# Waits on TensorE's own work behind 256-instruction borders, also at units that already wait for two operations

## The chip, the cores and the metric

The kernel runs on one core of a Trainium2 chip. The metric is the device time of one execution in microseconds; the median of the runs is compared, and one execution is profiled.

## The reference

Two layers run one behind the other on 2048 rows of width 512, in bfloat16.

```
h  = x + attention(layernorm(x), mem0, Wq, Wk, Wv, Wo)     # 64 segments of 32 rows, a recurrence
h2 = h + (gelu(layernorm(layernorm(h)) @ w1 + b1) @ w2 + b2)

for s in range(64):                       # 32 heads of 128 each
    hs = concat(mem, x[32*s : 32*s+32])   # 8 rows of memory, 32 rows of the segment
    q, k, v = hs@Wq, hs@Wk, hs@Wv
    p = softmax(mask(q k^T * 128**-0.5))
    o = (p v) @ Wo
    mem, out[s] = o[:8], o[8:]            # the memory rows go into the next segment
```

The 64 segments are a chain, as each needs the eight memory rows of the one before. The second layer needs only finished rows.

## The kernel before

**Units and streams.** The program builds no instruction directly. It records operations (here called units on TensorE: a small group of weight loads and matmuls), each with what it reads and writes and an estimated duration. `schedule` orders them by a simulation of the five engines with their dependences; `wire` gives each operation the list `waits`, the operations of other engines or DMAs whose semaphores it must wait for; `windows` delays some transfers that SyncE issues; `pauses`, the subject of this document, comes last. `emit` then writes each engine's stream: for each entry in `waits` a `wait_ge`, then the instructions of the unit, the last of which counts up the engine's semaphore if anybody waits for the unit.

**How a wait becomes an instruction.** In the built program the first wait of a TensorE unit's list rides on the unit's first weight load or matmul. The others stand ahead of it in semaphore instructions (the profile shows them as EVENT_SEMAPHORE at L627, the line of `wait_ge`), each of which holds two. One wait takes no semaphore instruction, two or three take one, four or five two: `len(o.waits) // 2`, as `align` counts them.

**The work of a segment on TensorE.** The names are those of the order tables in the kernel. Q0, K0, Q1, K1, V0 and V1 are the projections, in passes of 8 instructions, four passes each (L970 and L709; a pass takes 0.2157 us in the plan). SC0 and SC1 (L1167, 32 instructions) are scores of the memory's rows, for heads 0 to 15 and 16 to 31; VectorE and ScalarE make a softmax of them, which VectorE transposes into `PTC` (L1184). F is filler: work that doesn't depend on the recurrence (projections of later rows, the second layer's W1, the late rows' Wo). PV0 and PV1 (L1198, L1202, 20 instructions) multiply `PTC` by V, PVA (L1274, L1280, 40 instructions) does it for the segment's own rows. WO (L1314) is eight units of 16 instructions. SA (L1224, 64 instructions) makes the scores of the next segment's own rows. SC0 waits for VectorE's transpose of K (`KALL`, L1010) and for a copy of Q into `ZC` (L1039, mostly on GpSimd); PV0 and PV1 wait for `PTC` and for an evacuation of V (`VS`, ScalarE).

**Borders.** TensorE's instructions come from memory in pieces of 256; in this kernel a border lies behind every 256th instruction of its stream, counted from a fixed offset (`FETCH_AT`). `pads` inserts weight loads without effect, so that the borders fall at chosen units. `align` walks the stream, counts the instructions and the waits' semaphore instructions, and puts into `heads` the first unit that starts behind each border.

**Pauses.** Behind each border `pauses` goes through the units that begin within the next `PAUSE_IN` = 64 instructions. To up to `PAUSES` = 3 of them it gives a wait on TensorE's own semaphore: on the latest earlier TensorE unit that ends, in the plan, at least `PAUSE_US` = 0.5 us before the unit starts. Before the change it does so only at units that wait for nothing else: passes, filler and WO units, but not SC0, PV0, PV1 or PVA, each of which waits for two operations or more. In this kernel there are 153 borders and 423 such waits.

Of the kernel before, what the change touches and what calls it, by code (L numbers as in the profile page):

```python
# [160 lines left out]
class Sched:  # L161
# [230 lines left out]
    def pauses(self):  # L392

        self.align()
        pe = self.streams["pe"]
        ends = [o.start + o.dur for o in pe]
        for first in self.heads:
            n, i = 0, first
            while n < PAUSES and i < len(pe) and pe[i].at < pe[first].at + PAUSE_IN:
                o = pe[i]  # L400
                j = bisect.bisect_right(ends, o.start - PAUSE_US) - 1
                if not o.waits and 0 <= j < i:
                    o.waits = [pe[j]]
                    pe[j].sig = True
                    n += 1
                i += 1
        c = 0
        for o in pe:
            if o.sig:
                c += 1  # L410
                o.sigcount = c
# [1463 lines left out]
```

## Time and profile before

| what | value |
|---|---|
| three runs | 783.87, 784.82, 785.61 us; median 784.82 |
| the profiled execution | 784.86 us, of which 783.1 us is the span of the trace |
| granted TensorE clock in it | 1.00 |

Times in the views are microseconds from the start of the span. A row of the timeline is: start, duration, engine, line of the kernel, operation, what it writes and reads with shapes, and the number of instructions that the row stands for; in square brackets the idle time ahead of it and what ended it ("issue": nothing that the profile shows was waited for). PE is TensorE's matmul side, PEld its weight loads, PEldq semaphore instructions that stand ahead of weight loads, DVE VectorE, ACT ScalarE, POOL GpSimd, SP SyncE. A row of the semaphore instructions gives count, shortest/median/longest duration in ns, and when the first and the last of them started; a semaphore instruction is shown from the moment at which what it waits for is there. A row of the DMA queues gives the packets, the megabytes and the time that the packets took as a share of 16 engines; q8 is the queue that brings instructions.

### The profile page before, as it was taken

The numbers are of one execution on the slowest core, as the hardware profiler recorded it, in microseconds if no ns is written. First come the engines' busy times: TensorE is split into PE (matmuls) and PEld (weight loads), VectorE is DVE, ScalarE is ACT, GpSimd is POOL, SyncE is SP. The second block draws the span as 40 slices with busy tenths as digits, with TensorE's granted clock in tenths as the row PEclk, the third lists the DMA queues.
The fourth block names the chain that finished last, engine by engine and source line by source line (L and its number), as shares of the span: only waits on it lengthen the run. The fifth ranks groups of instructions, "written<-read, shape, count | busy, mean of one in ns | idle before, by whom it ended". The sixth has DMA issues, their size and how long they took to land.

```text
span 783.1 us, 44192 instructions
## 1 busy us (share of the span) xinstructions
PE 763.2 (97%) x19535; PEld 407.8 (52%) x19327; DVE 592.4 (76%) x1873; ACT 535.6 (68%) x1391; POOL 310.4 (40%) x830
## 2 busy tenths in 40 slices
PE   6979999999999999999999999999999999999898
PEld 2325555655655555655555555555555555554344
DVE  4458888888888888888888988888898777764311
ACT  3547777767677777777777777777767777776332
POOL 3012233444444444444444435443444434446600
PEclk9999999999999999999999999999999999999999
DMA  9973212020212111202020101111131120169510
GB/s 316 393 224 75 64 44 35 7 48 15 50 39 44 32 39 51 51 26 51 23 51 24 46 28 42 33 36 45 29 84 35 54 74 31 51 211 293 131 41 27
DMA packets 75915, 58.56 MB, mean 75 GB/s; under 512 B 31172, under 2 KB 68556, under 8 KB 75724
## 3 DMA queue, kind: packets, MB, share of 16 engines
q1 hardware_dynamic: 75392, 55.47, 25.2%
q8 instruction: 153, 2.51, 1.3%
q14 instruction: 38, 0.31, 0.1%
q10 hardware_dynamic: 332, 0.27, 0.1%
HBM read 37.63 MB, written 11.80 MB: 63 GB/s over the span
## 4 chain that ended last, share of the span: by engine, by line
PE 90%; SPq 6%; DVE 1%; DMA 1%; POOL 1%; issue 1%; ACT 0%; DVEq 0%; POOLq 0%
PE high L970 33%; PE high L709 17%; PE quad L1314 15%; PE quad L1743 4%; PE high L1521 3%; PE high L1353 3%; SPq L896 3%; PE high L1731 3%; SPq L871 2%; PE quad L1167 2%; PE quad L1224 2%; PE quad L1274 2%; PE quad L1198 2%; PE high L1198 1%; DMA WO<-in_A_Wo_dram 1%
## 5 line engine op out<-in xcount | busy, mean ns | idle before, releaser
L970 PE MATMUL high<-WQ,hT 128*32 128x512 bf16 x1796 | 156.3, 381 | 1.6 <-DVE hT L1320 1.2
L709 PE MATMUL high<-WK,hT 128*32 128x512 bf16 x1260 | 126.4, 379 | 0.2 <-issue 0.2
L988 ACT CAST kq<-high 128x512 bf16<-128x512 f32 x184 | 105.8, 583 | 30.0 <-PE high L970 18.4
L1314 PE MATMUL quad<-WO,OT 128*32 128x256 bf16 x4032 | 121.9, 273 | 0.0
L970 PE MATMUL high<-WV,hT 128*32 128x512 bf16 x1544 | 116.6, 379 | 0.0
L1247 POOL TENSOR_TENSOR PA<-SA,rsa 128x256 bf16<-128x256 f32 x64 | 39.6, 619 | 185.7 <-DVE rsa L1239 119.9
L1314 PEld LDWEIGHTS quad<-WO,OT 128*32 128x32 bf16 x4032 | 102.2, 97 | 5.3 <-issue 0.5
L989 ACT ACTIVATE kq<-high 128x512 bf16<-128x512 f32 x156 | 91.9, 598 | 15.6 <-PE high L970 12.4
L970 PEld LDWEIGHTS high<-WQ,hT 128*32 128x32 bf16 x1796 | 50.8, 95 | 73.1 <-issue 31.7
L1255 POOL COPY BD<-PTA 32x128 f32<-32x128 f32 x256 | 80.3, 314 | 16.3 <-DVE PTA L1251 0.6
L988 ACT CAST VS<-high 128x512 bf16<-128x512 f32 x127 | 73.7, 581 | 0.2 <-PE high L970 0.2
L1010 DVE STREAM_TRANSPOSE KALL<-kq 128x256 f32<-128x256 f32 x160 | 69.5, 435 | 4.1 <-ACT kq L988 1.2
L988 ACT CAST OT<-quad 128x384 bf16<-128x384 f32 (+1 forms) x126 | 47.2, 375 | 26.1 <-PE quad L1202 25.0
L1326 DVE STREAM_TRANSPOSE TT<-quad 128x256 f32<-128x256 f32 x63 | 28.3, 449 | 43.3 <-PE quad L1314 43.1
L1010 DVE STREAM_TRANSPOSE QT<-kq 128x256 f32<-128x256 f32 x128 | 54.8, 428 | 2.8 <-ACT kq L989 2.5
L970 PE MATMUL high<-WK,hT 128*32 128x512 bf16 x788 | 55.7, 379 | 1.0 <-DMA WK<-in_A_Wk_dram 1.0
L1050 ACT COPY KALL<-KALL 128x128 f32<-128x128 f32 x63 | 18.8, 298 | 53.0 <-PE quad L1224 51.8
L1366 POOL TENSOR_TENSOR opT<-TTB,TTS 32x64 bf16<-32x64 f32 x128 | 39.9, 312 | 37.1 <-DVE opT L1320 21.2
L968 PEld LDWEIGHTS <-hT 128*32 128x32 bf16 x2432 | 39.3, 96 | 27.9 <-DVE hT L1320 5.9
L1167 PEld LDWEIGHTS quad<-KALL,ZC 128*32 128x32 bf16 x1984 | 31.2, 96 | 43.0 <-POOL BD L1255 18.4
L709 PE MATMUL high<-WV,hT 128*32 128x512 bf16 x504 | 51.6, 379 | 0.0
L1182 DVE SCALAR_TENSOR_TENSOR PC<-EC,rsc,even 128x128 bf16<-128x128 f32 x126 | 46.4, 368 | 4.3
(204 smaller groups left out, 1588.0 us busy)
## 6 DMA issues: line engine op xcount, KB each, us to landing
WK<-in_A_Wk_dram SPq DMA_DIRECT2D x4, 1024.0 KB, 18.2
WQ<-in_A_Wq_dram SPq DMA_DIRECT2D x4, 1024.0 KB, 18.2
WO<-in_A_Wo_dram SPq DMA_DIRECT2D x16, 256.0 KB, 7.8
VBD<-v_last SPq DMA_DIRECT2D x60, 64.0 KB, 2.0
g_pre<-kq SPq DMA_DIRECT2D x14, 256.0 KB, 2.2
WV<-in_A_Wv_dram SPq DMA_DIRECT2D x3, 1024.0 KB, 11.3
VSB<-in_B_w_dram SPq DMA_DIRECT2D x44, 64.0 KB, 2.2
xr<-in_A_x_dram SPq DMA_DIRECT2D x17, 128.0 KB, 2.8
```

Source lines behind the costliest of these rows:

```text
L709: return e.add_instruction(mybir.InstMatmult(name="I-%d" % (4000000 + _kept[0]), engine=mybir.EngineType.PE, start_tensor_calc=start, stop ...
L968: e.ldweights(l, tile_position=(0, 32 * j))
L970: ins = e.matmul(o, l, m, start=(k == 0), stop=(k == DC - 1), tile_position=(0, 32 * j), skip_group_check=True)
L988: return {"act": (lambda e: e.copy(out, src), t_act(n, ps_)), "dve": (lambda e: e.tensor_copy(out, src), 0.155 + 1.0e-3 * n * fast)}
L989: return {"act": (lambda e: e.mul(out, src, scale_), t_act(n, ps_)), "dve": (lambda e: e.tensor_scalar(out, src, scale_, None, ALU.mult), ...
L1010: turn = lambda after: S.op("dve", lambda e: e.transpose(out, src), reads=[("kq", i)], writes=[key], dur=t_dve(256) + 0.02, after=after)
L1167: ins = e.matmul(o[32 * j:32 * j + 32, :], zc_window(h), rhs, start=False, stop=(i == 3), tile_position=(0, 32 * j), skip_group_check=True)
L1182: S.op("dve", lambda e: e.scalar_tensor_tensor(PC[:, r].rearrange("p k b -> p b k"), xc, rsc[:, r:r + 1], ev, ALU.mult, ALU.mult), reads=[ ...
L1247: S.either({k: ((lambda e: e.tensor_tensor(PA[:, 0:4].rearrange("p a t b -> p a b t"), SA[:, :, 0:SEG].rearrange("p (a b) t -> p a b t", b ...
L1255: S.narrow(S.op("pool", lambda e, j=j, rows=rows: e.tensor_copy(words(BD[rows, :, j, :, :]), words(PTA[rows, 0:4])), reads=["PTA"], writes ...
L1314: ins = e.matmul(ps[bank][32 * j:32 * j + 32, 0:256], lhs(slot(h)), wo_cols(h, b), start=(k == 0), stop=(k == 15), tile_position=(0, 32 * ...
L1366: return e.tensor_tensor(o[32 * q:32 * q + 32, c:c + 2], x, y, ALU.add)
```

## The change

In the profile's numbering the changed lines are in `pauses`:

```
             while n < PAUSES and i < len(pe) and pe[i].at < pe[first].at + PAUSE_IN:
                 o = pe[i]
                 j = bisect.bisect_right(ends, o.start - PAUSE_US) - 1
-                if not o.waits and 0 <= j < i:
-                    o.waits = [pe[j]]
+                if len(o.waits) % 2 == 0 and 0 <= j < i and not any(p.eng == "pe" and not p.is_dma for p in o.waits):
+                    o.waits = sorted(o.waits + [pe[j]], key=lambda p: p.start + p.dur + self.lat(p, o))
                     pe[j].sig = True
                     n += 1
```

A unit also gets the wait if it has two waits already (or four, or six), none of them on TensorE. The list with the new wait in it is sorted by the time at which each awaited operation is planned to be seen. The limit of three for each border stays, so a wait that is put on an earlier unit can take the place of one further on.

More of the change, by code (lines that the diff above doesn't have):

```diff
@@ L401, in pauses @@
                 j = bisect.bisect_right(ends, o.start - PAUSE_US) - 1
-                if not o.waits and 0 <= j < i:
-                    o.waits = [pe[j]]
+                if len(o.waits) % 2 == 0 and 0 <= j < i and not any(p.eng == "pe" and not p.is_dma for p in o.waits):
+                    o.waits = sorted(o.waits + [pe[j]], key=lambda p: p.start + p.dur + self.lat(p, o))
                     pe[j].sig = True
```

## The prediction

> **What bounds the kernel now.** I read the page first: the busy times, the chain that ended last, the DMA queues.
>
> ```profile
> span 783.1 us, 44192 instructions
> ...
> PE 763.2 (97%) x19535; PEld 407.8 (52%) x19327; DVE 592.4 (76%) x1873; ACT 535.6 (68%) x1391; POOL 310.4 (40%) x830
> ...
> q8 instruction: 153, 2.51, 1.3%
> ...
> PE 90%; SPq 6%; DVE 1%; DMA 1%; POOL 1%; issue 1%; ACT 0%; DVEq 0%; POOLq 0%
> ```
>
> TensorE is busy for 97% of the span and carries 90% of the chain; waits of other engines matter only through it. Queue q8 brings instructions: 153 packets of 2.51 MB / 153 = 16.4 KB, one for each border of the kernel's pieces (256 instructions at 64 bytes), each at work for 0.013 x 16 x 783.1 / 153 = 1.06 us. Then the windows view over the segments, and TensorE's timeline at one border inside them.
>
> ```profile
> 100.00:640.00 540.00, 538.85 (x15404) 299.52 (x15412) 462.34 (x1508) 397.54 (x1080) 233.22 (x640) 1.00 0.16 39
> ```
>
> ```profile
> 165.49 0.39 PE L709 MATMUL high<-WK,hT 128*32 128x512 bf16 x3
> 166.05 0.38 PE L709 MATMUL high<-WK,hT 128*32 128x512 bf16 x1 [0.17 <-issue]
> 166.09 0.55 PE L970 MATMUL high<-WQ,hT 128*32 128x512 bf16 x4
> ```
>
> In 540 us TensorE stands still for 1.15 us, at a granted clock of 1.00. So no wait for data is left to shorten there; what is left is stops like the one at 166.05: the stream reaches a border, nothing that a semaphore shows is late, and the next instruction comes late all the same ("issue"). The change touches nothing else that TensorE waits for, so its effect has to come through these stops, or through new stops of its own.
>
> **The change part by part.** It has three parts: 52 waits are added at 46 of the 153 borders (the lists walked by the new condition: 19 on SC0, 14 on PV1, 8 on PV0, 6 on PVA, 5 on single units at the two ends); 22 old ones fall out, since a border still gets three (17 on the third V0 pass behind an SC0); and the order of the waits at the changed units may shift.
>
> Instructions: none. A unit with two waits has one semaphore instruction ahead of it and one wait on its first weight load; the third wait goes into that same semaphore instruction, which holds two. So no border moves. I cost this at 0.
>
> SC0 (19). The unit at 455.80 stands for them.
>
> ```profile
> 454.94 0.83 PE L970 MATMUL high<-WK,hT 128*32 128x512 bf16 x12
> ...
> 455.80 0.31 PE L1167 MATMUL quad<-KALL,ZC 128*32 128x64 bf16 x16
> ```
> ```profile
> 455.00 0.45 DVE L1010 STREAM_TRANSPOSE KALL<-kq 128x256 f32<-128x256 f32 x1
> ```
> ```profile
> 455.04 0.29 POOL L1039 COPY ZC<-QT 128x128 bf16<-128x128 bf16 x1
> ```
>
> The added wait is on a unit inside the first row: the latest one that ends half a microsecond ahead of SC0 in the plan, about 455.34 by the trace. VectorE's transpose ends at 455.00 + 0.45 = 455.45, later. The wait is met before the old ones are: 0. The same holds for PV1, where the transposed PTC comes last, and for PVA, which stands behind PV0 in the stream.
>
> PV0 (8, seven of them with a fetch behind) is the exception.
>
> ```profile
> 171.47 0.40 PE L709 MATMUL high<-WK,hL 128*32 128x512 bf16 x4
> ...
> 171.90 0.40 PE L709 MATMUL high<-WK,hL 128*32 128x512 bf16 x4
> 172.23 0.26 PE L1198 MATMUL quad<-PTC,VS 64*128 64x16 bf16 x8
> ...
> 172.74 0.26 PE L1198 MATMUL high<-PTC,VS 64*128 64x16 bf16 x8
> ```
> ```profile
> 171.19 0.23 DVE L1184 STREAM_TRANSPOSE PTC<-PC 128x64 f32<-128x64 f32 x1
> ...
> 172.35 0.25 DVE L1184 STREAM_TRANSPOSE PTC<-PC 128x64 f32<-128x64 f32 x1
> ```
> ```profile
> L627 PEldq EVENT_SEMAPHORE  x3: 51/51/51, 171.4 to 171.7; - x3
> ```
> ```profile
> 109.30 0.40 PE L709 MATMUL high<-WV,hL 128*32 128x512 bf16 x4
> ```
> ```profile
> 109.23 0.24 DVE L1184 STREAM_TRANSPOSE PTC<-PC 128x64 f32<-128x64 f32 x1
> ```
> ```profile
> L627 PEldq EVENT_SEMAPHORE  x2: 51/51/51, 109.5 to 109.7; - x2
> ```
> ```profile
> 77.99 0.23 DVE L1184 STREAM_TRANSPOSE PTC<-PC 128x64 f32<-128x64 f32 x1
> ```
> ```profile
> 78.25 0.40 PE L709 MATMUL high<-WK,XX 128*32 128x512 bf16 x4
> ```
>
> At 172.23 the old wait, on PTC, is met at 171.19 + 0.23 = 171.42, and the gate (the semaphore instruction ahead of the unit) opens at 171.4. The new one, on the unit of 171.47, is met when that ends, 171.47 + 0.40 = 171.87: some 0.4 us later, 0.35 of it at the gate that opens last. At 110.06 the two ends are 109.47 and 109.70, and the gate opens 0.2 later; near 79, 78.22 and 78.65, 0.4 later. Of the seven, one is like 79, two like 172 (the other at 214) and four like 110 (141, 193 and 275 too, worked out in the same way): 0.4 + 2 x 0.35 + 4 x 0.2 = 1.9 us by which gates open later.
>
> Does this delay PV0 itself? A unit behind a gate can start 0.14 after its last operand is there: PTC's second half ends at 172.60 and PV1 starts at 172.74. The new gate opens 172.23 - 171.87 = 0.36 ahead of PV0, so the matmul is on time: 0 directly. Queued behind the wait on TensorE are PV0, PVA and the next projections; nobody else waits for them earlier than today.
>
> What the later gate may delay is the next fetch. The DMA queue view has no q8 packet in 109.7 to 110.6 nor in 171.8 to 172.6, and one in each of the next 0.2 us:
>
> ```profile
> q8 instruction: 1, 0.02, 30.7%
> ```
> ```profile
> q8 instruction: 1, 0.02, 38.3%
> ```
>
> These fetches start 1.1 to 1.2 us behind the first gate, as they do at the other five of these borders. If that is cause, each starts later by what its gate does. Who waits for it: the border after, in the SA unit that follows.
>
> ```profile
> 82.11 0.65 PE L1224 MATMUL quad<-KALL,QT 128*32 128x40 bf16 x32
> ```
> ```profile
> 113.09 0.40 PE L1224 MATMUL quad<-KALL,QT 128*32 128x40 bf16 x32
> ```
> ```profile
> 143.95 0.19 PE L1224 MATMUL quad<-KALL,QT 128*32 128x40 bf16 x4
> 144.39 0.36 PE L1224 MATMUL quad<-KALL,QT 128*32 128x40 bf16 x28 [0.25 <-issue]
> ```
> ```profile
> 175.17 0.69 PE L1224 MATMUL quad<-KALL,QT 128*32 128x40 bf16 x32
> ```
> ```profile
> 195.99 0.40 PE L1224 MATMUL quad<-KALL,QT 128*32 128x40 bf16 x32
> ```
> ```profile
> 216.92 0.41 PE L1224 MATMUL quad<-KALL,QT 128*32 128x40 bf16 x32
> ```
> ```profile
> 278.44 0.60 PE L1224 MATMUL quad<-KALL,QT 128*32 128x40 bf16 x32
> ```
>
> Undisturbed the unit takes 0.40. Four of the seven take 0.25, 0.40 (143.95 to 144.75), 0.29 and 0.20 more: those borders are already late, and take a later fetch whole: 0.4 + 0.2 + 0.35 + 0.2 = 1.15. The other three (113, 196, 217) have a slack that the trace does not show: between 0 and 0.2 + 0.2 + 0.35 = 0.75. I take 0.35, the middle, since the four neighbours show that the slack is small at best. Sum: 1.15 + 0.35 = 1.5, bounds 1.15 and 1.9.
>
> The 22 dropped waits. Seventeen are the third stop behind SC0; the first two V0 passes and SC0's gate keep theirs. Most of these fetches start 1.1 to 1.3 us behind SC0's gate, which stays: 0. Three start later, 282.8's among them:
>
> ```profile
> L627 PEldq EVENT_SEMAPHORE  x1: 51/51/51, 282.8 to 282.8; - x1
> ```
> ```profile
> L627 PEldq EVENT_SEMAPHORE  x1: 51/51/51, 284.2 to 284.2; - x1
> ```
> ```profile
> q8 instruction: 1, 0.02, 29.2%
> ```
>
> Here the packet is in 284.3 to 284.5, 1.5 or more behind the gate at 282.8 and 1.0 behind the last V0 stop. Without that stop it may come sooner (down to -0.4 us, which would win nothing, as the border behind is on time) or wait for the next one, SC1's gate at 284.2, and start about 1 us later. I take 0, as it is nearest to the other fourteen.
>
> [...]
>
> In all: 784.86 + 1.5 = 786.4 us. 784.86 is the profiled execution (span 783.1 and 1.8 around it); it lies 0.04 above the median of the runs, 784.82, so the forecast holds for either.
>
> **The rivals.**
>
> *The waits are redundant and nothing happens.* The fetch is set by when the border is crossed, or by the fetch before it, and the 1.1 us behind the gate is chance. For it: at 306, the eighth PV0, the packet is in the same 0.2 us as the gate opens, too soon to be its effect.
>
> ```profile
> L627 PEldq EVENT_SEMAPHORE  x2: 51/51/51, 305.5 to 305.7; - x2
> ```
> ```profile
> q8 instruction: 1, 0.02, 29.5%
> ```
>
> (the latter in 305.5 to 305.7). Against it: seven of seven earlier ones sit at 1.1 to 1.4 behind. The time is 784.9. [...]
>
> *The held stream lets the refill start sooner (the other side: faster).* Stops just behind a border give the fetch room; more of them would do more. It decides if a gate that stays shut frees the fetch at once rather than when it opens. Then the late borders behind changed ones vanish: 0.25 + 0.40 + 0.29 + 0.20 = 1.14, and some five like 166.05 (0.17 idle and a piece that ran late, about 0.2 each): 784.86 - 1.14 - 1.0 = 782.7; with the SA borders alone 783.7. Against it: SC0's and PV1's waits are met before the old ones, so they hold nothing; only PV0's do.
>
> *The dropped V0 waits cost.* As the forecast, and the three fetches wait for SC1's gate: 1 us later, less the 0.4 or so by which those borders have slack: 3 x 0.6 = 1.8. 784.86 + 1.5 + 1.8 = 788.2.
>
> **How the numbers follow.** Forecast 0.42, redundant 0.27, faster 0.16, dropped waits 0.15. A measurement of this kernel can tell about 0.2%, 1.57 us. The forecast's centre lies on that bound: half of it counts as same, half as slower. Same 0.27 + 0.21 = 0.48, slower 0.21 + 0.15 = 0.36, faster 0.16. Range: 783.4 (the SA borders alone less 0.3 for the spread of a run) to 788.4; it leaves out the stronger half of the faster case and the end of the last, about 0.15. The forecast's own range is 786.0 to 786.8.
>
> **What would show it.** PV0's gates near 110 and 172 open at 109.7 and 171.8 rather than 109.5 and 171.4, and the q8 packets come later by as much; SA takes 0.2 to 0.4 longer at 82, 144, 175 and 278. The gates of SC0 and PV1 stand where they stood, and q8 still has 153 packets. Wrong if: q8's packets stay in place (redundant), SA takes 0.40 throughout (faster), or new stops appear behind 284 (dropped).

## The result and the profile after

The change is slower: 792.11 us in the median (790.36 to 795.59) against 784.35 (783.55 to 785.61), a ratio of 1.0096 with a 95% interval of 1.0068 to 1.0124. By the ratio that is 7.5 us, where the forecast said 1.5 and its range ended at 788.4. The profiled execution took 792.78 us; its page:

```profile
span 791.0 us, 44192 instructions
...
PE 765.5 (97%) x19535; PEld 408.1 (52%) x19327; DVE 592.0 (75%) x1873; ACT 535.4 (68%) x1391; POOL 310.0 (39%) x830
...
q8 instruction: 153, 2.51, 1.4%
...
PE 89%; SPq 6%; issue 1%; DMA 1%; DVE 1%; POOL 1%; ACT 0%; DVEq 0%; POOLq 0%
```

Instructions, matmuls and fetches are as many as before: no border moved. TensorE's busy time grew by 2.3 us, the span by 7.9, so most of the loss is standing still. The waits view of TensorE over the whole span gives what ended the idle time, the total, how often, and the longest. First the kernel before, then the changed one (of each only the rows on idle time that nothing shown was waited for, above 0.4 us):

```profile
PE quad L1224 <- issue: 1.1, 2, 0.8
```
```profile
PE quad L1314 <- issue: 4.8, 5, 1.2
...
PE quad L1224 <- issue: 2.2, 6, 0.7
...
PE high L970 <- issue: 0.5, 2, 0.2
```

Two things are new. In SA (L1224) the stops grew from 1.1 to 2.2 us, which the forecast had. In WO (L1314) there are five stops of together 4.8 us, and before there was none. The groups of that line show the same (busy time, mean ns of one, idle time ahead), before and after:

```profile
L1314 PE MATMUL quad<-WO,OT 128*32 128x256 bf16 x4032 | 121.9, 273 | 0.0
```
```profile
L1314 PE MATMUL quad<-WO,OT 128*32 128x256 bf16 x4032 | 122.8, 273 | 4.8 <-issue 4.8
```

With the 0.9 us by which the busy time grew these are 5.7 us. One of the five stops, in segment 23, by its timeline:

```profile
288.20 0.84 PE L970 MATMUL high<-WK,hT 128*32 128x512 bf16 x12
288.85 0.41 PE L709 MATMUL high<-WV,hT 128*32 128x512 bf16 x4
289.06 0.30 PE L1167 MATMUL quad<-KALL,ZC 128*32 128x64 bf16 x15
...
292.57 0.40 PE L1314 MATMUL quad<-WO,OT 128*32 128x256 bf16 x8
294.21 0.62 PE L1314 MATMUL quad<-WO,OT 128*32 128x256 bf16 x16 [1.24 <-issue]
```

The semaphore instructions between 288.7 and 290.6 (the gates of SC0 and SC1), and the one instruction packet that the DMA queue view has between 288.7 and 291.5, in its last 0.2 us:

```profile
L627 PEldq EVENT_SEMAPHORE  x2: 51/51/51, 288.9 to 290.2; - x2
```
```profile
q8 instruction: 1, 0.02, 38.8%
```

In the kernel before this fetch started 1.5 us behind SC0's gate (282.8 and 284.3, quoted in the prediction). Now it starts 2.4 us behind it, 1.2 behind SC1's gate, and at the border in WO that follows TensorE stands for 1.24 us, until 2.8 us after the fetch's start. The same is to be seen in segments 7, 17, 20 and 56; the five fetches start 2.45 to 3.0 us behind SC0's gate, 0.9 to 1.8 later than before.

PV0 near 175 is the one that the prediction follows at 172. Its first row is the unit that the new wait is on; PV0's gate; SA behind it:

```profile
174.59 0.40 PE L709 MATMUL high<-WK,hL 128*32 128x512 bf16 x4
...
175.35 0.26 PE L1198 MATMUL quad<-PTC,VS 64*128 64x16 bf16 x8
```
```profile
L627 PEldq EVENT_SEMAPHORE  x2: 51/51/51, 174.6 to 175.0; - x2
```
```profile
178.94 0.36 PE L1224 MATMUL quad<-KALL,QT 128*32 128x40 bf16 x28 [0.45 <-issue]
```

The gate opens at 175.0, 0.35 ahead of PV0 and not 0.8; the q8 packet is in 176.2 to 176.4, again 1.2 behind the gate; PV0 is on time; SA stands for 0.45 us. At this border the part went as forecast. Over all seven its sum did so too, but not its terms. Behind PV0 of segments 3, 6 and 9 the SA units look like this:

```profile
84.55 0.21 PE L1224 MATMUL quad<-KALL,QT 128*32 128x40 bf16 x6
85.46 0.35 PE L1224 MATMUL quad<-KALL,QT 128*32 128x40 bf16 x26 [0.70 <-issue]
```
```profile
115.97 0.21 PE L1224 MATMUL quad<-KALL,QT 128*32 128x40 bf16 x5
116.34 0.35 PE L1224 MATMUL quad<-KALL,QT 128*32 128x40 bf16 x27 [0.16 <-issue]
```
```profile
147.39 0.39 PE L1224 MATMUL quad<-KALL,QT 128*32 128x40 bf16 x32
```

From the first matmul to the last, SA takes 0.61 us more than before in segment 3 (forecast 0.4), 0.31 in 12 (0.35) and 0.02 in 22 (0.2). In segment 9 it takes 0.41 less, where 0.2 more was forecast: its fetch starts as the gate opens, and no longer 1.2 us behind it. These four together add 0.5 us and not 1.15. The three borders with slack (segments 6, 14 and 16) add 0.3 each, together 0.95, where the prediction took 0.35 and set the bound at 0.75.

2.2 of the 7.9 us between the two profiled executions can't be put down to the change. The matmuls of the scores behind the opening start at 55.9 us before and at 58.1 after, as the source view of their line has it, while the waits listed for the opening are the same ones:

```profile
L1167 PE MATMUL quad<-KALL,ZC x288: 189/193/205, 55.9 to 139.6; 128*32 128x64 bf16 x144
```
```profile
L1167 PE MATMUL quad<-KALL,ZC x256: 189/193/204, 58.1 to 132.9; 128*32 128x64 bf16 x128
```

The change alters four waits of the opening, but six of the twelve kernels below leave TensorE's opening as it was (`e3_pv0`, `f2_early`, `f3_pv0_early`, `g1_last`, `g3_ahead`, `g4_ahead_late`), and in them that start lies anywhere from 56.1 to 58.2: it scatters by itself. The profiled execution of before had the earliest of all.

### The profile page after: what moved, and what is told of

It reads as the page before. It is cut to its first block, busy times and chain, and to the rows that moved or that the text cites. A ratio compares the mean times of both kernels' runs of the same rounds, so it can differ in the third digit from the quotient of the medians.

```text
span 791.0 us, 44192 instructions
## 1 busy us (share of the span) xinstructions
PE 765.5 (97%) x19535; PEld 408.1 (52%) x19327; DVE 592.0 (75%) x1873; ACT 535.4 (68%) x1391; POOL 310.0 (39%) x830
## 3 DMA queue, kind: packets, MB, share of 16 engines
q8 instruction: 153, 2.51, 1.4%
## 4 chain that ended last, share of the span: by engine, by line
PE 89%; SPq 6%; issue 1%; DMA 1%; DVE 1%; POOL 1%; ACT 0%; DVEq 0%; POOLq 0%
PE high L970 33%; PE high L709 17%; PE quad L1314 15%; PE quad L1743 4%; PE high L1353 4%; PE high L1521 3%; SPq L896 3%; PE high L1731 3%; SPq L871 2%; PE quad L1167 2%; PE quad L1224 2%; PE quad L1274 2%; PE quad L1198 2%; PE high L1198 1%; DMA WO<-in_A_Wo_dram 1%
## 5 line engine op out<-in xcount | busy, mean ns | idle before, releaser
L1314 PE MATMUL quad<-WO,OT 128*32 128x256 bf16 x4032 | 122.8, 273 | 4.8 <-issue 4.8
L1314 PEld LDWEIGHTS quad<-WO,OT 128*32 128x32 bf16 x4032 | 102.0, 97 | 11.0 <-issue 6.2
```

Source lines behind the costliest of these rows:

```text
L1314: ins = e.matmul(ps[bank][32 * j:32 * j + 32, 0:256], lhs(slot(h)), wo_cols(h, b), start=(k == 0), stop=(k == 15), tile_position=(0, 32 * ...
```

## The experiments

All twelve differ only in which TensorE units get a wait on an earlier TensorE unit, or on which; no instruction is added and no border moves. Three theories stood at the start: D, the stop dropped behind SC0 (the third behind the border) lets fetches miss their turn; S, the new wait at SC0 does it; P, PV0's later gate delays the chain of fetches and so makes the one behind SC0 miss. Ratios are to the kernel before on the same chip, with 95% intervals; its medians there were 785.1, 784.2 and 785.95 us.

**The change taken apart.** `e1_keep` counts the plain and the mixed stops apart, so that the 22 old ones stay:

```
+ some = len(o.waits) % 2 == 0 and 0 <= j < i and not any(p.eng == "pe" and not p.is_dma for p in o.waits)
+ if some and (not o.waits and n < PAUSES or o.waits and m < PAUSES):
+     n += not o.waits
...
+ m += some
```

> All 52 added waits, and the 22 old ones that fell out kept beside them. Theory D (the dropped third stop behind SC0 lets five fetches miss their turn, 5.9 us by the borders behind them, and PV0's later gates cost some 1.3): 785.7. Rival S (the added wait at SC0 itself makes the fetches late): about 790.5. Rival P (PV0's later gate delays the next fetch, and this makes the fetch behind SC0 miss; it holds for three of the five, with PV0's own 1.3 about 5): about 789.

Measured: 786.87 us, ratio 1.0022 (1.0002 to 1.0041). Of the change's 7.5 us 1.7 are left, as D has it.

`e2_drop` adds the wait only `if some and not o.waits`, and counts `n += some`.

> No wait added; the 22 that the change drops are dropped. Theory D: about 790.3 (784.4 and the 5.9 of the five late borders), the fetches behind SC0 in segments 7, 17, 20, 23 or 56 start behind SC1's gate. Rival S: 784.4. Rival P: 2.1 (the two late borders that do not follow a PV0 with the added wait) and so 786.5.

Measured: 791.70 us, ratio 1.0082 (1.0052 to 1.0113): dropping alone costs 6.4 us. The fetches behind SC0 are late in six segments (7, 15, 17, 20, 23, 56), and six stops in WO carry it (its line is 1315 here):

```profile
PE quad L1315 <- issue: 5.2, 6, 1.2
```

`e3_pv0` is `e1_keep` with `o.waits and m < PAUSES and o.tag and o.tag[1] == "PV0"`, and `e4_rest` the same with `not (o.tag and o.tag[1] == "PV0")`.

> Only the eight waits at PV0 added, nothing dropped. Theory D, and the forecast's own sum: 784.4 + 1.3 = 785.7, SA in segments 3 to 22 up to 0.4 later, fetches behind SC0 in place. Rival S: 785.7 too. Rival P: the fetches behind SC0 in segments 7, 17 and 23 are late as well, about 789.

> The 44 added waits that are not at PV0 (19 at SC0, 14 at PV1, 6 at PVA, 5 others), nothing dropped. Theory D: 784.4, no difference. Rival S: about 790. Rival P: 784.4.

Measured: `e3_pv0` 787.29 us, ratio 1.0026 (1.0009 to 1.0044), and no fetch behind SC0 late; `e4_rest` 785.17 us, ratio 1.0001 (0.9984 to 1.0019). The other 44 waits cost nothing, so S falls. P falls as well: with PV0's later gates and the third stops in place the fetches of segments 7, 17 and 23 are in time. In the trace of `e4_rest` one fetch behind SC0, in segment 52, starts 3.35 us behind the start of the gate's instruction though all three stops are there, the only one of its kind in the fourteen traces. The gates of SC0 and SC1, and the copy into `ZC` that SC0 waits for:

```profile
L629 PEldq EVENT_SEMAPHORE  x2: 51/460/870, 579.3 to 581.2; - x2
```
```profile
579.79 0.29 POOL L1041 COPY ZC<-QT 128x128 bf16<-128x128 bf16 x1
```

With the added wait SC0's semaphore instruction holds two waits, and here it lasts 870 ns and not 51: the trace shows it from 579.3, while the copy is late in this execution and ends at 580.08, so the gate opens 0.8 us later than its start says. The last stop had opened at 579.8, ahead of that, and the fetch starts 2.5 us behind the gate's opening, 1.45 behind SC1's gate. So it is one more late fetch whose last stop opened too early, here because the gate was late: 0.3 us ahead of it.

SA's stops in `e3_pv0` (line 1226 there):

```profile
PE quad L1226 <- issue: 3.2, 7, 0.7
```

**Why the third stop matters.** The dropped stop could count as one of three, by its place, or because it is the last to open. `f1_late` is the whole change, with the dropped stops still dropped, and one line ahead of its condition, by which the wait goes to the unit after:

```
+ j += o.tag is not None and o.tag[1] == "V0"
```

> The whole change, with the same 22 waits dropped, but every wait at a V0 pass goes to the TensorE unit after the one that the change takes, so that the last stop behind SC0 opens some 0.2 us later (in segments 7, 17, 20, 23 and 56 at 0.28 to 0.33 behind SC0's gate rather than 0.07 to 0.14). Theory T (what counts is how long the stream is still held behind SC0's gate): the late fetches come back to 1.1 to 1.8 us behind the gate and the time is that of the change without its drops, 787. Rival N (what counts is the number of stops, or how far behind the border the last one stands): 791 to 792, as the change.

Measured: 786.47 us, ratio 1.0028 (1.0011 to 1.0044), no fetch late. The stops are as few and at the same units as in the change; those at V0 passes only open 0.2 us later.

`f2_early` is the kernel before, all three stops at their units, with `j -= ...` in place of `j += ...`.

> No wait added or dropped, but every wait at a V0 pass goes to the TensorE unit before the one that the kernel before takes, so that the last stop behind SC0 opens some 0.2 us earlier, at about 0.14 behind SC0's gate where SC0 stands six to eighteen instructions behind the border and at 0.3 elsewhere less 0.2. Theory T: fetches behind SC0 start behind SC1's gate, in at least the five or six segments of the kernel that only drops, perhaps in all seventeen: 790 or more. Rival N: 785.

Measured: 791.11 us, ratio 1.0079 (1.0056 to 1.0102), the same six fetches late as when the third stops are dropped. Segment 23 once more, first in `f1_late`. Its last stop waits for the second of these passes; then the gates of SC0 and SC1, the fetch (in 287.2 to 287.4), and WO:

```profile
285.17 0.84 PE L971 MATMUL high<-WK,hT 128*32 128x512 bf16 x12
285.81 0.41 PE L710 MATMUL high<-WV,hT 128*32 128x512 bf16 x4
...
289.54 1.06 PE L1315 MATMUL quad<-WO,OT 128*32 128x256 bf16 x32
```
```profile
L628 PEldq EVENT_SEMAPHORE  x2: 51/51/51, 285.9 to 287.2; - x2
```
```profile
q8 instruction: 1, 0.02, 32.3%
```

The same of `f2_early`, whose last stop waits for the end of the first row; the fetch is in 289.6 to 289.8. Its waits view stands last:

```profile
286.53 0.83 PE L971 MATMUL high<-WK,hT 128*32 128x512 bf16 x12
...
292.24 0.82 PE L1315 MATMUL quad<-WO,OT 128*32 128x256 bf16 x21 [0.95 <-issue]
```
```profile
L628 PEldq EVENT_SEMAPHORE  x2: 51/51/51, 287.2 to 288.5; - x2
```
```profile
q8 instruction: 1, 0.02, 31.4%
```
```profile
PE quad L1315 <- issue: 5.8, 6, 1.2
```

In the first the stop opens at 285.81 + 0.41 = 286.22, 0.3 behind SC0's gate, and the fetch starts 1.3 behind it. In the second it opens at 286.53 + 0.83 = 287.36, a bare 0.1 behind the gate, the fetch starts only behind the next gate (289.6 or later, the gate at 288.5), and WO stands for 0.95 us. `f1_late` has no row for WO in its waits view. Number and place of the stops speak against the outcome in both kernels; the time at which the last one opens goes with it in both.

`g1_last` is the kernel before with only the last of the stops at V0 passes, 32 fewer:

```
+ v = [o for o, _ in some if o.tag and o.tag[1] == "V0"]
+ for o, p in some:
+     if o not in v[:-1]:
+         o.waits = [p]
+         p.sig = True
```

> The kernel before with 32 stops fewer: of the stops at V0 passes behind a border only the last is kept, nothing added. Theory T (only how long the stream is held behind SC0's gate counts): no difference, 785, and all fetches behind SC0 within 1.1 to 1.8 us of the gate. Rival N (the number of stops counts): late fetches as in the change, 790 or more.

Measured: 785.01 us, ratio 0.9996 (0.9974 to 1.0018), no fetch late. One stop does what three did, if it opens late enough.

**PV0's part.** `f3_pv0_early` is `e3_pv0` with `j -= 1` at PV0 and the wait put at the end of the list, so that it stands in the semaphore instruction.

> Only the eight waits at PV0, in the semaphore instruction ahead of it as in the change, but each on the TensorE unit before: it ends some 0.2 us ahead of the transposed PTC, or with it. If PV0's cost lies in the time at which its gate opens: 785, as before. If it lies in a third wait in the list: 787.3, as with the waits of the change.

Measured: 785.01 us, ratio 1.0006 (0.9992 to 1.0019). The same third wait, met 0.4 us earlier, costs nothing that can be measured. Its interval overlaps that of `e3_pv0`, which ran on another chip, so the times alone don't decide; the traces do. SA's stops, 3.2 us in `e3_pv0`, are here (line 1228):

```profile
PE quad L1228 <- issue: 0.6, 1, 0.6
```

So the cost lies in the time at which the gate opens.

`g2_both` is the whole change with both shifts:

```
+ j += (name == "V0") - (name == "PV0")
```

PV0's wait stands at the end of the list, as in `f3_pv0_early`.

> The whole change with both repairs: waits at V0 passes on the unit after, waits at PV0 on the unit before. If the two causes found are all there is, it is as before, 785; what is left over 785 is a third cause.

Measured: 785.89 us, ratio 0.9999 (0.9979 to 1.0018). Two shifts of one unit each take the whole loss away; no third cause is left that can be measured. Against `f1_late` (1.0028), which lacks PV0's shift alone, this is PV0's part once more.

**Looking for a faster one.** `f4_five` is the kernel before with `PAUSES = 5`. `g3_ahead` begins two units ahead of the border where the first unit behind it is filler (`n, i = -2, first - 2`), and `g4_ahead_late` adds the line of `f1_late` to it.

> The kernel before with up to five stops behind a border instead of three, within the same 64 instructions, none at a unit that waits for something else; 130 more stops. If longer holding always helps, the 4.9 us of late borders shrink and it is 782 to 784. If the holds that are there are enough: 785. If more stops delay work: over 786.

> The kernel before with up to two more stops ahead of the borders whose first unit is filler, on the two units that begin before the border. If a longer hold behind SC1's gate lets those fetches take SC1's turn as in the later segments (1.2 to 1.5 us behind its gate rather than 2.1 to 2.5), the SA borders of segments 3 to 22 are in time and it is 783 to 784. If the hold has to lie behind the border, 785.

> The same, and every wait at a V0 pass on the unit after, so that the holds behind SC0 have more to spare. If both count, the lowest of all, 783; if the kernel before loses nothing behind SC0, as g3.

Measured: `f4_five` 785.28 us, ratio 1.0008 (0.9992 to 1.0025); `g3_ahead` 784.93 us, 0.9991 (0.9967 to 1.0014); `g4_ahead_late` 783.63 us, 0.9978 (0.9958 to 0.9998). More stops don't help by themselves. Stops ahead of the border missed their aim: in the trace of `g3_ahead` the fetches of segments 3, 6, 12, 14, 16 and 22 still start 2.2 to 2.8 us behind SC1's gate. The last one is 0.2% below the kernel before, with an interval that only just leaves out 1; why it should win is not settled, as the profiled execution of before has no late fetch behind SC0 for the later stops to save, and with twelve kernels tried one such interval may be chance.

## Why the prediction was wrong

**What bounds the kernel: right.** The loss came through borders at which TensorE stands with nothing shown to wait for, and no other loss is left when these are repaired (`g2_both`).

**Instructions, SC0, PV1, PVA: right.** 44192 instructions and 153 fetches as before; `e4_rest` puts these waits at 1.0001.

**PV0: right in mechanism; the size is in part luck.** The gates open later by what was worked out, the fetches follow, SA stands longer, PV0 itself is on time. Forecast 1.5 us; alone it measures 1.0026 x 785.1 - 785.1 = 2.0 us (0.7 to 3.5), with all waits kept 1.7. In the trace of the changed kernel the seven SA units take 0.5 + 0.95 = 1.5 us more, the forecast's figure, but from other terms (1.15 + 0.35): that two misses of opposite sign cancel is luck. `f3_pv0_early` against `e3_pv0` shows that the time at which the gate opens counts (SA's stops are 0.6 and 3.2 us), and with it rules out the redundant rival; only where PV0 stands 24 instructions behind the border (segments 9 and 25) does the fetch start with the gate in some traces and 1.2 to 1.3 us behind it in others, and why is open. That the crossing sets the fetch, as that rival had it, the runs contradict: waits behind the crossing moved the five late ones by 0.9 to 1.8 us.

**The 22 dropped waits: this step failed.** "I take 0, as it is nearest to the other fourteen": the reason was that most fetches start 1.1 to 1.3 us behind SC0's gate, which stays. They do, but, segment 13 apart, only where the last stop opened 0.17 us or more behind that gate. Nor is it so that the first two V0 passes keep their stops everywhere: in segments 4, 17, 20 and 56 one is left and in 57 none, and three of the five late fetches are among these. What follows is about the seventeen borders with SC0 at most 18 instructions behind them (those of the seventeen dropped stops, with segment 13 in place of 57, where the fetch starts ahead of SC0's gate). In the kernel before the last stop opens 0.26 to 0.59 us behind the gate, and no fetch of seventeen is late. Without the third stop it opens at 0.06 to 0.37, and the late ones are those at the low end: all seventeen late fetches of the changed kernel, `e2_drop` and `f2_early` had a last stop that opened at most 0.14 behind the gate. Only segment 13 was in time with 0.05 to 0.14, in six kernels; why it is an exception is open. The dropped stops measure 1.0082, 6.4 us, where 0 stood in the sum.

The rival "the dropped waits cost" had what happened, the fetch that comes only behind SC1's gate (1.2 us behind it in segment 23), but a wrong size and the wrong borders. Of the three fetches that it feared for (segments 23, 28 and 62, which started late behind SC0's gate already) only that of segment 23 was hit; four were hit that had started at 1.2 to 1.4. And the price of each was taken as 1 us less a slack of 0.4, while the five took 5.7 / 5 = 1.1 us each, slack and all.

The dropped stops ride on weight loads. `f1_late` against the change (1.0028 and 1.0096), and `f2_early` against the kernel before (1.0079), move nothing but such waits, by one pass, and move the fetch with them: in segment 23 it starts 1.3 us behind SC0's gate in `f1_late` and 2.4 in the change, 1.5 in the kernel before and 2.4 in `f2_early`. So here a wait on a weight load does count, as far as fetches are concerned.

**The faster rival: wrong.** The borders that it would have saved stayed late or moved about (only segment 9's was saved); where one hold opened later, at PV0, the next fetch came later, too.

What was shown is that the time of the last stop decides: one unit later or earlier took the ratio from 1.0096 to 1.0028 (`f1_late`) and from 1 to 1.0079 (`f2_early`). What happens in those 0.2 us no run shows.

## What to carry to other kernels

A wait that does no work in the profile, on an operation long done, was here what kept an instruction fetch in time: 22 dropped cost 6.4 us (`e2_drop`), and 32 fewer cost nothing that can be measured where the last to open stayed (`g1_last`, 0.9996). Before one is dropped, even as a side effect of a limit on their number, look at when the stream is released last, not at how many stops there are. When a rule for such waits is widened, count what it pushes out as carefully as what it adds; here the added waits cost 2 us and the displaced ones 6. It matters, too, which unit such a wait is on. At PV0, which waits for something else already, the unit to take was one that ends before that is there; at the V0 passes behind SC0 it was the later one. One unit was worth 0.2 to 0.3% at PV0 and 0.7 to 0.8% at V0.

## What the runs showed of the hardware

The profiled executions of the kernel before and of the change show 153 packets of 2.51 MB / 153 = 16.4 KB on q8. In the second TensorE has 19535 matmuls, 19327 weight loads and 345 semaphore instructions of L627: 39207 / 153 = 256 for each packet.

Behind the seventeen borders just ahead of SC0, the next fetch started 1.1 to 1.8 us behind SC0's gate in the kernel before. Where it missed that, it started 1.0 to 1.6 us behind the next gate, which opened 1.1 to 1.4 us later. What went with the one or the other was when the last wait on TensorE's own work that rides on a weight load behind the gate was met: 0.17 us behind the gate's opening or later, or 0.14 or less. That is from the seventeen late fetches of the changed kernel, `e2_drop` and `f2_early`. One case stands against it: segment 13, in time with 0.05 to 0.14. In segment 10 of the changed kernel the fetch started 0.7 us ahead of the gate, with no late border behind it.

A late fetch showed at the border after it. In the 45 stops of more than 0.3 us in SA and WO that the fourteen traces hold, TensorE went on 2.2 to 3.0 us after the start of the last fetch ahead of the stop, though the packet itself was at work for only 0.9 to 1.5 us.

A semaphore instruction with two waits of which one was met later stood in the trace from about the one's end to about the other's: for 870 ns in `e4_rest`, and for 147 to 242 at six in the changed kernel, where the median of all 345 is 51. One of these, PV0's gate at 112.39, lasted 242 ns; the two operations that it waits for ended at 112.12 + 0.24 = 112.36 and 112.18 + 0.40 = 112.58:

```profile
112.12 0.24 DVE L1184 STREAM_TRANSPOSE PTC<-PC 128x64 f32<-128x64 f32 x1
```
```profile
112.18 0.40 PE L709 MATMUL high<-WV,hL 128*32 128x512 bf16 x4
```
```profile
L627 PEldq EVENT_SEMAPHORE  x1: 242/242/242, 112.4 to 112.4; - x1
```
